# Attention transposes in 64-row halves, and a planner that counts 512-column evacuations as longer

## The chip, the cores and the metric

One core of one Trainium2 chip runs the whole program. The metric is the device time of that core in microseconds, the median of several executions.

## The reference

Causal block attention (blocks of 64) over 8 batches, 8 heads, 576 positions and head size 64, then a layer norm, a two-layer ReLU network of width 2048 and a residual, all in fp32:

```
scores = q @ k.T / sqrt(D), masked so that block i sees blocks j <= i
attn   = exp(scores - max) / (sum + 1e-9)
x      = attn @ v                       # heads side by side: 512 columns
xn     = (x - mean) / sqrt(var + 1e-6) * g_ln
out    = x + max(xn @ w_ch1, 0) @ w_ch2
```

## The kernel before, in words

**Two stages.** The attention runs over 32 pairs of heads (`pair`, line 396), with a short extra piece for the first block of every second batch (`first`, line 552, after pairs 3, 11, 19 and 27). Then the network runs over rounds of row tiles (`products` and `second`), and is one long stream of matmuls. Its weights arrive as 64-bit words, which `decode` turns into fp32 on ACT, DVE and POOL while the attention runs, and the first row tiles are normalised (`norm_tiles`, `operands`) there as well. This is the filler of DVE and ACT.

**One pair.** TensorE makes the scores of the two heads in 64-row mode, one head on the upper 64 rows of the array and one on the lower: first the small blocks into two `s1` banks (S1, 512 columns per head), then the large ones into two double banks `s` (S0, 1024 columns per head). DVE reads each score block once (line 443, a custom operation that masks, copies to SBUF and takes the row's extreme): four operations per S1 (320, 192, 320, 192 columns into `pu`), four per S0 (576 and 448 for each head into `pab`). They are called softenings here. ACT takes exponentials in place (line 446). TensorE turns the exponentials (`turn`, line 451): eight cells of 128x128 of `pu` in two banks, sixteen of `pab` in four banks, four cells to a bank. Each bank is then copied to SBUF by DVE or ACT (`evac`, line 387; the copies stand at L236 for DVE and L234 for ACT) into `pt1` and `pt0`. Then the products with V follow (`pv`, lines 461 and 465): PV1 reads `pt1`, PV0 reads `pt0`, both write bank `o`, which DVE transposes out (line 539, `ot`).

**PSUM.** The `s1`, transposed, `o` and `p` tiles share four banks under one tag, `tr`, and take them in turn: per pair two for `s1`, six for the transposes, one for `o`. The `s` tiles have four banks of their own.

**What sets the order.** `Plan` (line 61) is a list scheduler that runs when the program is built. Every piece of work is a task with a cost per engine; some may go to DVE or ACT (`any_of`), and it takes the engine that it expects to be done first. Its output is a fixed order per engine; at run time an engine waits where a semaphore says so. The attention's TensorE work is put in one fixed chain by `pe(at, phase, ...)` and `plan.chain`: in step k come S1(k), S0(k), then the transposes of pair k-1 for `pt1` (T1) and `pt0` (T0), then PV1(k-1) and PV0(k-1). A 512-column evacuation is counted by `dve(n)` and `act(n)`:

```
def dve(n):
    return .07 + n / 960
def act(n, sbuf=False):
    return .055 + .085 * sbuf + n / 1200
```

The planner's cost of one transposed cell is .112 (`4 * .112` per bank), and `SWITCH` adds a cost when TensorE changes between 128-row work, 64-row work and the column halves of the V products.

Of the kernel before, what the change touches and what calls it, by code (L numbers as in the profile page):

```python
# [18 lines left out]
P = 128  # L19
# [4 lines left out]
BIAS = {'PE': 0, 'SP': 0, 'DVE': 0, 'ACT': 0, 'POOL': 0}  # L24
WARM = 12
MMO = .0134
ROUNDS = 8, 8, 8, 8, 4
TILES = sum(ROUNDS)
D_0, D_1 = 12.0, .97
# [28 lines left out]
class Plan:  # L58
# [5 lines left out]
    def add(self, eng, cost=None, fn=None, r=(), w=(), prio=0.0, size=0, alloc=(), mode=128):  # L64
        k = Task(eng if isinstance(eng, dict) else {eng: (cost, fn)}, prio, size)
        k.mode = mode
        before = {}
        for x in r:
            before.update(dict.fromkeys(x.writers))
        for x in w:  # L70
            before.update(dict.fromkeys(x.readers))
        for x in r:
            x.readers.append(k)
        for x in w:
            x.writers.append(k)
        for x in before:
            x.next.append(k)
        k.left = len(before)
        k.uses = list(dict.fromkeys(x.root for x in (*r, *w, *alloc)))
        for x in k.uses:  # L80
            x.users += 1
        k.allocs = [x for x in dict.fromkeys(x.root for x in (*w, *alloc)) if x.make]
        self.tasks.append(k)
        return k
# [105 lines left out]
# [6 lines that stand above are left out]
# [6 lines left out]
def attn_mlp_kernel(ctx: ExitStack, tc: tile.TileContext, qk, qk0, v, v0, w1, w2, g, out):  # L202
# [8 lines left out]
    nc = tc.nc  # L211
# [12 lines left out]
    add = plan.add  # L224
# [3 lines left out]
    def any_of(fn, **costs):  # L228

        return {e: (c, lambda e=e: fn(engines[e])) for e, c in costs.items()}  # L230

    def copy(e, out, in_):
        if e is nc.scalar:
            e.copy(out=out, in_=in_)  # L234
        else:
            e.tensor_copy(out, in_)  # L236
# [37 lines left out]
    new_tr, new_s1, new_o, new_p = (kind(n, [P, 512], F32, 4, psum, "tr") for n in ("tr", "s1", "o", "p"))  # L274
# [37 lines left out]
    ident = odd.tile([P, P], F32, name="ident")  # L312
# [72 lines left out]
    HALF = slice(0, 64), slice(64, 128)  # L385

    def evac(out, in_, n, **kw):
        add(any_of(lambda e: copy(e, out(), in_()), DVE=dve(n), ACT=act(n)), **kw)

    def pe(at, phase, *args, **kw):  # L390
        steps.setdefault((at, phase), []).append(add("PE", *args, **kw))
# [3 lines left out]
    def pair(k):  # L395
        b, c = k // 4, k % 4
        prio = 100 + 10 * k
        step = [0]

        def pr():  # L400
            step[0] += 1
            return prio + .05 * step[0]
# [5 lines left out]
        else:  # L408
            early, late = Buf(parent=raw), Buf(parent=raw)
            for to, at, boxes in ((early, 30, ((slice(0, P), 0, 64, 320), (HALF[0], 1, 256, 576), (HALF[1], 1, 0, 320))),  # L410
                                  (late, 20, ((slice(0, P), 0, 320, 576), (HALF[0], 1, 0, 256), (HALF[1], 1, 320, 576)))):
                for rows, m, lo, hi in boxes:
                    load((rows.stop - rows.start) * (hi - lo) * 4, lambda rows=rows, m=m, lo=lo, hi=hi: nc.sync.dma_start(
                        out=raw.t[rows, m, lo:hi], in_=qk[k][rows, m, lo:hi]), w=[to], alloc=[raw], prio=prio - at)
# [12 lines left out]
        def cell(i, h, ck):  # L427

            at = FIRST[i] + (128 * i if ck == 0 else 128 * (i + ck) if h else 128 * (i - ck))
            return slice(at, at + P)  # L430
# [20 lines left out]
        def turn(o, slots):  # L451

            def go():
                for n, x in enumerate(slots()):
                    nc.tensor.transpose(o.t[:, n * P:(n + 1) * P], x, ident)  # L455
            return go

        def pv(o, at, z, steps):
            def go():
# [12 lines left out]
        pu = new_pu()  # L472
# [6 lines left out]
        low = [[], []]  # L479
# [5 lines left out]
        pab = big_of[k, 0] = new_pab()  # L485
# [8 lines left out]
        done = [[], []]  # L494
# [3 lines left out]
        pt0 = big_of[k, 1] = new_pt0()  # L498
        final[k] = [*done[0], *done[1]]
        got = []  # L500

        for h in range(2):
            for i in (4, 3):
                o, x = new_tr(), Buf(parent=pt0)
                if i == 4:
                    cells = [(4, h, ck) for ck in range(1, 5)]
                    need = [done[h][0]]
                else:
                    cells = [(3, h, ck) for ck in range(1, 4)] + [(3 + h, h, 0)]
                    need = [done[h][1]] + [done[x][1 - h] for x in range(2)]  # L510
                slots = lambda cells=cells: [pab.t[:, cell(*x)] for x in cells]
                pe(k + 1, 3, 4 * .112, turn(o, slots), r=list(dict.fromkeys(need)), w=[o], alloc=[pt0], prio=pr())
                evac(lambda h=h, i=i: pt0.t[:, h, :, i - 3], lambda o=o: o.t.rearrange("p (c n) -> p c n", c=4), 512,
                     r=[o], w=[x], prio=pr())
                got.append(x)
        ob, part_o = new_o(), []
        part_o.append(Buf(parent=ob))
        pe(k + 1, 5, (4 * 256 + 128) * 4 / 2400 + .06, pv(
# [2 lines left out]

        pt1 = new_pt1()
        got = []
        for h in range(2):
            o, x = new_tr(), Buf(parent=pt1)

            cells = (1, h, 1), (2, h, 1), (1 + h, h, 0), (2, h, 2)
            slots = lambda cells=cells: [pu.t[:, cell(*x)] for x in cells]
            need = low[h] + [low[x][1 - h] for x in range(2)]
            pe(k + 1, 2, 4 * .112, turn(o, slots), r=list(dict.fromkeys(need)), w=[o], alloc=[pt1], prio=pr())  # L530
            evac(lambda h=h: pt1.t[:, h].rearrange("p c i n -> p (c i n)"), lambda o=o: o.t, 512, r=[o], w=[x], prio=pr())
            got.append(x)
        part_o.append(Buf(parent=ob))
        pe(k + 1, 4.5, (2 * 256 + 128) * 4 / 2400 + .06, pv(
            ob, 0, lambda: pt1.t[:, :, 1, 0],
# [4 lines left out]
        rows = Buf(parent=xd[b])  # L540
# [98 lines left out]
    n = 0  # L639
# [388 lines left out]
```

## Time and profile before

| what | value |
|---|---|
| median of 3 runs | 1050.25 us (1049.67 to 1051.68) |
| span of the profiled execution | 1051.5 us (no other time of it is listed) |
| TensorE (PE) busy | 99% |
| VectorE (DVE) busy | 71% |
| ScalarE (ACT) busy | 50% |
| GpSimd (POOL) busy | 27% |
| mean granted TensorE clock | 0.996 |

The page's busy share of PE says that it almost never sits idle; it doesn't say whether its order could be shorter. The slices of the page show two different stages: over the first third ACT and DVE are at 7 to 9 tenths, afterwards at 2 to 4 and 5 to 6. So the stages have to be read apart, the first one step by step.

### The profile page before, as it was taken

How to read it: one execution, taken by the hardware profiler on the slowest of the kernel's cores; microseconds unless marked ns; L12 is line 12 of the kernel's file. 1: busy time of each engine (PE TensorE's matmuls, PEld its weight loads, DVE VectorE, ACT ScalarE, POOL GpSimd, SP SyncE). 2: the span in 40 equal slices, each digit the busy share in tenths (PEclk: the TensorE clock that was granted, in tenths of full speed). 3: DMA queues.
4: the chain of work that ended last, by engine and by line, in shares of the span. 5: the costliest groups of instructions: out<-in, count | busy, mean ns of one | idle time of the engine just before them, and what ended most of it. 6: DMA issues, size and time to landing. Idle time of an engine off the chain costs nothing.

```text
span 1051.5 us, 18007 instructions
## 1 busy us (share of the span) xinstructions
PE 1039.6 (99%) x6264; PEld 855.0 (81%) x6264; DVE 743.6 (71%) x1631; ACT 525.0 (50%) x1264; POOL 285.8 (27%) x468
## 2 busy tenths in 40 slices
PE   9999999999999999999999999999999999999998
PEld 7887777777778888888888888888888888888997
DVE  5878999789978878885656694665685565465544
ACT  7999897889984544441433341343242322122221
POOL 0223354445433755340222240222231220000000
PEclk9999999999999999999999999999999999999999
DMA  7678889898779898758787747688657667336873
GB/s 274 205 252 265 223 282 258 226 288 291 282 255 293 299 324 240 231 215 255 225 254 208 220 179 252 186 233 261 182 190 260 217 190 248 143 111 246 299 282 123
DMA packets 238682, 248.88 MB, mean 237 GB/s; under 512 B 159488, under 2 KB 189184, under 8 KB 228352
## 3 DMA queue, kind: packets, MB, share of 16 engines
q1 hardware_dynamic: 238592, 247.74, 73.1%
q8 instruction: 49, 0.80, 0.3%
q14 instruction: 41, 0.34, 0.1%
HBM read 182.68 MB, written 65.01 MB: 236 GB/s over the span
## 4 chain that ended last, share of the span: by engine, by line
PE 90%; DVE 6%; DMA 2%; ACT 1%; issue 1%; SPq 0%; POOL 0%; DVEq 0%; ACTq 0%; POOLq 0%
PE y L938 36%; PE p L876 32%; PE tr L455 7%; PE s L425 7%; PE o L465 5%; PE o L461 3%; DVE pab L443 1%; DMA x<-xd 1%; DMA was<-wa 1%; DVE pu L443 0%; DMA xrow<-x 0%; DVE ya L950 0%; DVE x L733 0%; DVE x L678 0%; DVE sgn L359 0%
## 5 line engine op out<-in xcount | busy, mean ns | idle before, releaser
L938 PE MATMUL y<-wc,h 128*128 128x512 f32 (+1 forms) x1740 | 434.0, 388 | 0.2 <-DVE h L896 0.2
L938 PEld LDWEIGHTS y<-wc,h 128*128 128x128 f32 x1740 | 323.0, 188 | 66.1 <-DVE h L896 1.3
L950 DVE TENSOR_TENSOR ya<-y,ya 128x512 f32<-128x512 f32 x290 | 198.0, 684 | 183.6 <-PE y L938 182.1
L876 PE MATMUL p<-xm,wa 128*128 128x512 f32 (+1 forms) x960 | 221.7, 368 | 0.0
L876 PEld LDWEIGHTS p<-xm,wa 128*128 128x128 f32 x960 | 169.9, 188 | 31.5 <-issue 0.2
L876 PE MATMUL p<-xm,wb 128*128 128x512 f32 (+1 forms) x720 | 166.3, 368 | 0.0
L884 ACT COPY t<-p 128x512 f32<-128x512 f32 (+1 forms) x120 | 65.3, 544 | 168.6 <-PE p L876 166.8
L876 PEld LDWEIGHTS p<-xm,wb 128*128 128x128 f32 x720 | 127.7, 188 | 23.6
L895 ACT ACTIVATE h<-t 128x512 fp32r<-128x512 f32 (+1 forms) x120 | 62.2, 579 | 163.5 <-DVE t L889 163.2
L889 DVE TENSOR_TENSOR t<-p,t 128x512 f32<-128x512 f32 (+1 forms) x120 | 76.3, 636 | 48.1 <-PE p L876 43.3
L425 PE MATMUL s<-raw 64*128 64x224 f32 (+3 forms) x768 | 97.6, 389 | 1.7 <-DVE nm L443 1.2
L234 ACT COPY pt<-tr 128x512 f32<-128x512 f32 x166 | 87.4, 597 | 9.1 <-PE tr L455 8.0
L446 ACT ACTIVATE pab<-pab,nm 128x448 f32<-128x448 f32 (+1 forms) x128 | 91.1, 730 | 0.1
L425 PEld LDWEIGHTS s<-raw 64*128 64x128 f32 x768 | 75.3, 189 | 17.8 <-issue 5.0
L443 DVE CUSTOM_DVE_ANT_0 pab<-s,never 128x448 f32<-128x448 f32 (+1 forms) x128 | 82.7, 684 | 2.5 <-PE s L425 1.9
L465 PE MATMUL o<-pt,v 128*64 128x256 f32 (+1 forms) x768 | 80.6, 345 | 0.0
L465 PEld LDWEIGHTS o<-pt,v 128*64 128x64 f32 x768 | 55.7, 138 | 28.3 <-issue 1.1
L896 DVE SCALAR_TENSOR_TENSOR h<-t,h 128x512 fp32r<-128x512 f32 (+1 forms) x120 | 74.1, 668 | 3.9 <-ACT h L895 3.8
L353 POOL TENSOR_SCALAR mag<-mag 128x512 f32<-128x512 f32 x32 | 48.7, 1523 | 100.0 <-ACT mag L350 92.1
L690 POOL TENSOR_SCALAR norm<-norm 128x1 f32<-128x1 f32 x28 | 7.2, 258 | 248.9 <-ACT xn L687 248.9
L446 ACT ACTIVATE pu<-pu,nm 128x320 f32<-128x320 f32 (+1 forms) x128 | 64.7, 509 | 19.9 <-DVE nm L443 18.9
L455 PE MATMUL tr<-ident,pab 128*128 128x128 f32 x512 | 65.0, 279 | 5.1 <-DVE nm L443 4.2
(96 smaller groups left out, 1035.6 us busy)
## 6 DMA issues: line engine op xcount, KB each, us to landing
wc<-wcs SPq DMA_DIRECT2D x40, 1024.0 KB, 7.1
wa<-was SPq DMA_DIRECT2D x32, 1024.0 KB, 6.4
wb<-wbs SPq DMA_DIRECT2D x32, 768.0 KB, 5.5
raw<-qk SPq DMA_DIRECT2D x31, 576.0 KB, 4.9
wr<-w SPq DMA_DIRECT2D x32, 512.0 KB, 6.2
v<-v SPq DMA_DIRECT2D x32, 320.0 KB, 5.2
x<-xd SPq DMA_DIRECT2D x144, 64.0 KB, 4.0
xrow<-x SPq DMA_DIRECT2D x36, 256.0 KB, 4.2
```

The source lines that it names most:

```text
L234: e.copy(out=out, in_=in_)
L425: nc.tensor.matmul(x, raw.t[HALF[h], 0, col], raw.t[HALF[h], 1, at:at + x.shape[1]], start=True, stop=True)
L443: add("DVE", dve(n) + .01, lambda: nc.vector.tensor_tensor_reduce(out=two(p.t[:, part(i, h)]), in0=mine(), in1=two(hide), scale=-0.125, sc ...
L446: add("ACT", act(n, True) + .14, lambda: nc.scalar.activation(out=p.t[:, part(i, h)], in_=p.t[:, part(i, h)], func=AF.Exp, bias=nm.t[:, at ...
L455: nc.tensor.transpose(o.t[:, n * P:(n + 1) * P], x, ident)
L465: nc.tensor.matmul(o.t[HALF[h], at + lo:at + 256], v_sb.t[:, ck, HALF[h]], rhs(h), start=False, stop=(n == len(steps) - 1), skip_group_che ...
L876: nc.tensor.matmul(x.t[:, 0:TN], w_(l), xs[m].t[:, 0:half, o, k], start=start and k == e == 0, stop=k == 1 and e == 2, skip_group_check=True)
L884: add("ACT", act(TN), lambda: nc.scalar.copy(out=t.t[:, 0:TN], in_=x.t[:, 0:TN]), r=[r], w=[new], prio=0)
L889: add("DVE", dve(TN), lambda: nc.vector.tensor_add(t.t[:, 0:TN], x.t[:, 0:TN], t.t[:, 0:TN]), r=r, w=[new], prio=0)
L896: add("DVE", dve(TN), lambda: nc.vector.scalar_tensor_tensor(out=x.t[:, 1, 0:TN], in0=src(), scalar=0.0, in1=x.t[:, 0, 0:TN], op0=ALU.max, ...
L938: nc.tensor.matmul(yb.t[:, cut], x.t[:, l, at:at + P], wc.t[:, i, o, cut], start=i == e == 0, stop=i == 1 and e == 2, skip_group_check=end)
L950: add("DVE", dve(cut.stop - cut.start), lambda yb=yb, ya=ya, cut=cut: nc.vector.tensor_add(ya.t[:, cut], yb.t[:, cut], ya.t[:, cut]), r=[p ...
```

## The change

The transposes go over to half cells. Each 128x128 cell becomes two matmuls in 64-row mode: the upper 64 rows (64 queries) times a 64x64 identity into one bank, the lower 64 rows into another, 64 columns each. A bank now holds one half of eight cells, so a group of eight cells fills two banks together, and there are three groups per pair: `pu` (T1), head 0 of `pab` (T0a) and head 1 (T0b). The copies still read 512 columns each, six per pair, and write runs of 64 columns. For the planner, a group costs 8 cells at .112 and is in mode 64 like the scores, and a 512-column evacuation lasts .08 (DVE) or .115 (ACT) longer than before. These costs enter the choice between DVE and ACT, and with it the order of everything else on the two engines.

```diff
 MMO = .0134
+TURN = .112
@@
     def evac(out, in_, n, **kw):
-        add(any_of(lambda e: copy(e, out(), in_()), DVE=dve(n), ACT=act(n)), **kw)
+        add(any_of(lambda e: copy(e, out(), in_()), DVE=dve(n) + .08, ACT=act(n) + .115), **kw)
@@
             def go():
                 for n, x in enumerate(slots()):
-                    nc.tensor.transpose(o.t[:, n * P:(n + 1) * P], x, ident)
+                    for rows, to in zip(HALF, o):
+                        nc.tensor.transpose(to.t[:, 64 * n:64 * n + 64], x[rows], ident[rows, rows])
             return go
+
+        def turned_to(pt, at, o, x, to):
+            for q, src in enumerate(o):
+                x.append(Buf(parent=pt))
+                evac(lambda q=q: to()[..., 64 * q:64 * q + 64],
+                     lambda src=src: src.t.rearrange("p (c i q) -> p c i q", c=4, q=64), 512, r=[src], w=[x[-1]], prio=at)
@@
         for h in range(2):
-            for i in (4, 3):
-                o, x = new_tr(), Buf(parent=pt0)
...
-                pe(k + 1, 3, 4 * .112, turn(o, slots), r=list(dict.fromkeys(need)), w=[o], alloc=[pt0], prio=pr())
-                evac(lambda h=h, i=i: pt0.t[:, h, :, i - 3], lambda o=o: o.t.rearrange("p (c n) -> p c n", c=4), 512,
-                     r=[o], w=[x], prio=pr())
-                got.append(x)
+            o = [new_tr(), new_tr()]
+            cells = [x for c in range(3) for x in ((3, h, c + 1), (4, h, c + 1))] + [(3 + h, h, 0), (4, h, 4)]
+            slots = lambda cells=cells: [pab.t[:, cell(*x)] for x in cells]
+            need = [*done[h], done[1 - h][1 - h]]
+            pe(k + 1, 3, 8 * TURN, turn(o, slots), r=list(dict.fromkeys(need)), w=o, alloc=[pt0], prio=pr(), mode=64)
+            turned_to(pt0, pr(), o, got, lambda h=h: pt0.t[:, h])
@@
-        for h in range(2):
-            o, x = new_tr(), Buf(parent=pt1)
...
+        o = [new_tr(), new_tr()]
+        cells = [x for h in range(2) for x in ((1, h, 1), (2, h, 1), (1 + h, h, 0), (2, h, 2))]
+        slots = lambda: [pu.t[:, cell(*x)] for x in cells]
+        pe(k + 1, 2, 8 * TURN, turn(o, slots), r=[*low[0], *low[1]], w=o, alloc=[pt1], prio=pr(), mode=64)
+        turned_to(pt1, pr(), o, got, lambda: pt1.t.rearrange("p h c i n -> p (h c) i n"))
```

Over the whole program the planner gives DVE 67 of the 196 evacuations where it had 30, and ACT 129 where it had 166. TensorE gets 1,536 transposes of 128x64 (128 output partitions, 64 columns) in place of 768 of 128x128. Three places show what moved.

TensorE, step 17 of the attention, from the last scores to the first products with V (first before, then changed; `x8` counts like instructions, `s<-raw` are scores, `o<-pt` products with V):

```order
L425 MATMUL s<-raw 128x224 x4
L455 MATMUL tr<-ident,pu 128x128 x8
L455 MATMUL tr<-ident,pab 128x128 x16
L461 MATMUL o<-pt_2161,v 64x256 x2
L465 MATMUL o<-pt_2161,v 64x256 x2
```

```order
L426 MATMUL s<-raw 128x224 x4
L457 MATMUL tr<-ident,pu 128x64 x16
L457 MATMUL tr<-ident,pab 128x64 x32
L469 MATMUL o<-pt_2558,v 64x256 x2
L473 MATMUL o<-pt_2558,v 64x256 x2
```

The chain is the same; each transpose has become two of half the columns.

DVE, the same step 17, the softenings of S0 and what stands around them (first before, then changed; `ISA pab` is a softening, `ISA nm` its row extreme, `COPY pt` an evacuation, `sgn` and `wd` weight decoding):

```order
L443 ISA pab,nm<-s,never 128x576
L443 ISA nm 128x1
L443 ISA pab,nm<-s,never 128x448
L443 ISA nm 128x1
L443 ISA pab,nm<-s,never 128x576
L443 ISA nm 128x1
L236 COPY pt_2178<-tr 128x4x128
L443 ISA pab,nm<-s,never 128x448
L443 ISA nm 128x1
L359 SCALAR_TENSOR_TENSOR sgn<-wr,sgn 128x512
L362 SCALAR_TENSOR_TENSOR sgn<-mag,sgn 128x512
L236 CAST wd<-sgn 128x512
```

```order
L360 SCALAR_TENSOR_TENSOR sgn<-wr,sgn 128x512
L444 ISA pab,nm<-s,never 128x576
L444 ISA nm 128x1
L237 COPY pt_2558<-tr 128x8x64
L444 ISA pab,nm<-s,never 128x448
L444 ISA nm 128x1
L444 ISA pab,nm<-s,never 128x576
L444 ISA nm 128x1
L237 COPY pt_2582<-tr 128x8x64
L444 ISA pab,nm<-s,never 128x448
L444 ISA nm 128x1
L363 SCALAR_TENSOR_TENSOR sgn<-mag,sgn 128x512
```

DVE has one evacuation among the S0 softenings before, and two in the changed order: one of T1 (`pt_2558`) and one of T0 (`pt_2582`), and a piece of decoding stands ahead of them.

DVE again, step 26, from the first softening of S0 to `ot` (first before, then changed):

```order
L443 ISA pab,nm<-s,never 128x448
L443 ISA nm 128x1
L236 COPY pt_3388<-tr 128x4x128
L443 ISA pab,nm<-s,never 128x576
L443 ISA nm 128x1
L443 ISA pab,nm<-s,never 128x448
L443 ISA nm 128x1
L359 SCALAR_TENSOR_TENSOR sgn<-wr,sgn 128x512
L362 SCALAR_TENSOR_TENSOR sgn<-mag,sgn 128x512
L236 CAST wd<-sgn 128x512
L539 STREAM_TRANSPOSE ot<-o 128x512
```

```order
L444 ISA pab,nm<-s,never 128x576
L444 ISA nm 128x1
L444 ISA pab,nm<-s,never 128x448
L444 ISA nm 128x1
L444 ISA pab,nm<-s,never 128x448
L444 ISA nm 128x1
L237 COPY pt_4006<-tr 128x8x64
L444 ISA pab,nm<-s,never 128x576
L444 ISA nm 128x1
L237 COPY pt_4006<-tr 128x8x64
L536 STREAM_TRANSPOSE ot<-o 128x512
```

Here the second of two evacuations of `pt0` stands behind all four softenings; before, the only one stood behind two.

## Rows read from the trace of the kernel before

**Rows 1.** Busy time by stage (--windows): attention steps 1 to 30, and everything behind.
```profile
core 0: us, PE busy (x) PEld busy (x) DVE busy (x) ACT busy (x) POOL busy (x), PEclk, DMA share, GB/s
8.33:294.34 286.01, 279.30 (x2673) 220.14 (x2673) 246.97 (x743) 257.48 (x699) 105.88 (x134) 0.99 0.83 262
310.70:1051.50 740.80, 737.14 (x3416) 616.29 (x3414) 482.56 (x849) 250.38 (x525) 173.27 (x323) 1.00 0.70 228
```

**Rows 2.** TensorE in time (--timeline), step 17: start, length, line, tile, count.
```profile
156.18 2.86 PE L425 MATMUL s<-raw 64*128 64x320 f32 x24
158.97 1.09 PE L455 MATMUL tr<-ident,pu 128*128 128x128 f32 x8
159.90 1.91 PE L455 MATMUL tr<-ident,pab 128*128 128x128 f32 x16
161.74 0.65 PE L461 MATMUL o<-pt,v 128*64 128x256 f32 x4
162.88 0.60 PE L461 MATMUL o<-pt,v 128*64 128x256 f32 x4
163.31 1.68 PE L465 MATMUL o<-pt,v 128*64 128x256 f32 x16
164.92 2.86 PE L425 MATMUL s<-raw 64*128 64x320 f32 x24
```

**Rows 3.** Who waited for whom, 8 to 306 us: total us, times, longest.
```profile
DVE ot L539 <- PE o L465: 24.2, 21, 2.7
...
PE tr L455 <- DVE nm L443: 4.2, 3, 1.7
```

**Rows 4.** Groups by line and form: busy us, mean ns of one, idle before.
```profile
L455 PE MATMUL tr<-ident,pab 128*128 128x128 f32 x512 | 65.0, 279 | 5.1 <-DVE nm L443 4.2 <-ACT pt L234 0.6 <-DVE pt L236 0.3
...
L577 PE MATMUL tr<-qk 64*64 64x64 f32 x128 | 2.8, 224 | 0.0
...
L425 PEld LDWEIGHTS s<-raw 64*128 64x128 f32 x768 | 75.3, 189 | 17.8 <-issue 5.0 <-DVE ot L539 1.2 <-DVE nm L443 1.1
...
L236 DVE COPY pt<-tr 128x512 f32<-128x512 f32 x29 | 20.0, 689 | 9.1 <-PE tr L455 8.6 <-PE tr L606 0.2
...
L234 ACT COPY pt<-tr 128x512 f32<-128x512 f32 x165 | 86.9, 596 | 9.1 <-PE tr L455 8.0 <-issue 0.2
```

**Rows 5.** DVE in time, from step 17 into step 18.
```profile
159.07 0.76 DVE L443 CUSTOM_DVE_ANT_0 pab<-s,never 128x576 f32<-128x576 f32 x1
...
159.75 0.62 DVE L443 CUSTOM_DVE_ANT_0 pab<-s,never 128x448 f32<-128x448 f32 x1
...
160.30 0.75 DVE L443 CUSTOM_DVE_ANT_0 pab<-s,never 128x576 f32<-128x576 f32 x1
...
161.41 0.69 DVE L236 COPY pt<-tr 128x512 f32<-128x512 f32 x1 [0.35 <-PE tr L455]
162.02 0.61 DVE L443 CUSTOM_DVE_ANT_0 pab<-s,never 128x448 f32<-128x448 f32 x1
...
162.56 0.69 DVE L359 SCALAR_TENSOR_TENSOR sgn<-wr,sgn 128x512 int32<-128x512 int32 x1
...
165.04 0.72 DVE L539 STREAM_TRANSPOSE ot<-o 128x512 f32<-128x512 f32 x1
166.08 0.49 DVE L443 CUSTOM_DVE_ANT_0 pu<-s,never 128x320 f32<-128x320 f32 x1 [0.33 <-PE s L425]
...
167.47 0.69 DVE L362 SCALAR_TENSOR_TENSOR sgn<-mag,sgn 128x512 int32<-128x512 int32 x1
```

**Rows 6.** ACT in time, step 17: four evacuations in one row.
```profile
159.72 2.05 ACT L234 COPY pt<-tr 128x512 f32<-128x512 f32 x4
```

**Rows 7.** Busy time (--windows, columns as in rows 1) of two long steps, 19 and 20.
```profile
173.66:187.11 13.45, 11.40 (x115) 8.47 (x113) 9.82 (x32) 9.10 (x27) 6.00 (x17) 0.87 1.01 343
187.11:200.05 12.94, 11.06 (x86) 8.38 (x80) 10.26 (x31) 9.59 (x23) 6.46 (x5) 0.87 0.73 164
```

More of the change, by code (lines that the diff above doesn't have):

```diff
@@ L502, in pair @@
         for h in range(2):
-            for i in (4, 3):
-                o, x = new_tr(), Buf(parent=pt0)
[L505 to L511, printed above, removed]
-                pe(k + 1, 3, 4 * .112, turn(o, slots), r=list(dict.fromkeys(need)), w=[o], alloc=[pt0], prio=pr())
-                evac(lambda h=h, i=i: pt0.t[:, h, :, i - 3], lambda o=o: o.t.rearrange("p (c n) -> p c n", c=4), 512,
-                     r=[o], w=[x], prio=pr())
-                got.append(x)
+            o = [new_tr(), new_tr()]
[4 more added lines that the diff above has]
+            turned_to(pt0, pr(), o, got, lambda h=h: pt0.t[:, h])
         ob, part_o = new_o(), []
@@ L523, in pair @@
         got = []
-        for h in range(2):
-            o, x = new_tr(), Buf(parent=pt1)
[L527 to L532, printed above, removed]
+        o = [new_tr(), new_tr()]
[3 more added lines that the diff above has]
+        turned_to(pt1, pr(), o, got, lambda: pt1.t.rearrange("p h c i n -> p (h c) i n"))
         part_o.append(Buf(parent=ob))
```

## The prediction

> **What bounds the kernel now.** I read the stages first. Behind the attention TensorE is busy for 737.14 of 740.80 us [rows 1], so the end moves by what the attention gains or loses. Steps 1 to 30 of the attention take 286.01 us [rows 1], 9.53 each.
>
> Then one step in time [rows 2]. Step 17 lasts 8.74 us (156.18 to 164.92) and TensorE goes through it without a gap: scores 2.79, transposes 2.77, PV1 1.14, PV0 2.04. PV0 starts 6.70 after the step does. This is TensorE's own pace. The thirty steps are 24 us longer than 30 x 8.74; that is the extra piece of `first` (eight steps) and steps in which DVE comes late. Steps 19 and 20 alone take 13.45 and 12.94 [rows 7], and TensorE's largest wait is for softenings, 4.2 us [rows 3].
>
> Then the two engines that feed TensorE. DVE is busy for 247 and ACT for 257 of the 286 us [rows 1], so neither has much to spare. But their instructions overlap: a DVE copy is 0.69 long and its follower starts 0.61 after it (161.41, 162.02) [rows 5]; four ACT copies take 2.05, and with 0.60 for one that is 0.48 from start to start [rows 4, 6]. In the same way a softening of 576 columns occupies DVE for 0.68, one of 448 for 0.54, the four of S1 for 1.39 (166.08 to 167.47), decoding for some 0.66 [rows 5]. DVE's largest wait is for the products with V, 24.2 us in 21 waits [rows 3]. So in a normal step TensorE bounds, with DVE close behind.
>
> **The transposes themselves.** Sixteen cells take 1.91 us, one 0.28, so a cell costs (1.91 - 0.28) / 15 = 0.109 [rows 2, 4]. A 64-column matmul is 0.224 long against 0.279 for 128 columns [rows 4]: 64 columns save 0.055 and so cost about that. Two halves in the two row halves of the array can run side by side, as the scores do: 24 matmuls of 192 to 320 columns between 156.18 and 158.97 take 0.116 each [rows 2], where one alone, at 0.109 for 128 columns, would need at least 0.16. So the bounds for a cell are 0.055 (full overlap) and 0.109 (no gain). I take 0.058, nearest to the 64-column row: 24 cells in 1.4 us in place of 2.77. The scores and transposes are now in one mode; 24 x 0.109 = 2.62 of 2.77 leaves 0.15 for the changes of mode and the first load, of which I take 0.1 off. TensorE alone would save 1.5 us a step, 44 us in all.
>
> A rule speaks against this. The Trainium skill, page "TensorE: Matmul & The Clock Gate", section Part 2 (LDWEIGHTS), says that a weight load costs by its columns and not by its rows; half cells would then need twice the load time. The trace has 768 loads of 64 rows and 189 ns that keep their port busy for only 75.3 us, 98 ns each [rows 4], so loads of two row halves overlap; by the rule without overlap the sum would be that of the last rival below.
>
> **Where the saving stops.** Three groups of eight cells fill two banks each, and there are four banks, two of which hold `s1` until it is softened. So T0b cannot start before both copies of T1 are out, and PV0 not before the last copy. I walk step 17 in its changed order, from the start of S1. The S1 softenings start at 1.16 (166.08 - 164.92) and end at 2.55 [rows 2, 5]. The piece of decoding now ahead of S0's brings 3.21 (without it they would start at 2.89, as 159.07 - 156.18). Then 0.68 to 3.89, the T1 copy to 4.50, 0.54, 0.68 to 5.72, and the T0 copy to 6.33 [rows 5]; its data is out 0.08 later, and with the signal PV0 starts at 6.46. ACT, with four copies of 0.48 [rows 6], is through at 5.8. T0b runs from 4.6 to 5.1 and PV1 from 5.2 to 6.35, both in time. PV0 takes 2.04: the step lasts 8.50, not 7.2. The gain is 0.24.
>
> In step 26 DVE has all four softenings and two copies of T0 behind each other: 2.89 + 0.68 + 0.54 + 0.54 + 0.61 + 0.68 + 0.61 = 6.55, PV0 at 6.69, the step 8.73: no gain. From the first S0 softening to the last copy DVE now needs 3.0 to 3.3 us in ten of the thirty steps, about 3.7 in ten, 4.7 in one, and under 2.6 in nine, where ACT's copies or work ahead of the softenings decide.
>
> **The load.** DVE gets 37 evacuations more, 37 x 0.61 = 22.6 us; ACT loses 37 x 0.48 = 17.8. With what else changes place (three more weight words are decoded before the last `ot`, some casts go to ACT and POOL, which is at 106 of 286 us [rows 1] and costs nothing), DVE's own work in steps 1 to 30, by the counts of the two orders and the start-to-start times, goes from 234 to 251 us. No transfer is added. To the 251 come two waits that the chain forces on DVE in each step: 2.55 to 2.89, and about 0.4 between `ot` and the next S1 softening. That is 251 + 30 x 0.75 = 274, the floor for the thirty steps.
>
> **The sum.** I added up all thirty steps like step 17: PV0 starts at the latest of TensorE's own chain (6.1 now, 6.70 before), DVE's and ACT's; a DVE that ends a step late starts the next one late; `first` adds 0.6 to 1.1 in eight steps. This gives 269 for the order before, against 286.0 measured, and 276 for the changed one. Of the 17 that it misses before, 8.3 are in steps 19 and 20, where the granted clock was 0.87 [rows 7]: 0.13 x 26.4 = 3.4 us by the clock, the rest by late softenings, which in the changed order are already in the 276. I add 3.4 for the clock, 2.4 for the slow first step, 2 for small waits: 284, a gain of 2. At the end two more transposes are shorter by 1.4 each, and the order fills TensorE's waits there with products of the network: 2.5. Together 4.5 off the profiled 1051.5, so 1047.0; the median of the runs stands 1.25 below that profile. I predict **1046**.
>
> **The rivals.**
> - Forecast, a small gain: TensorE's saving is caught by the DVE chain, with 2 to 8 us left. For it: PV0 at 6.46 and 6.69 in the two walks. Against: the walk missed 17 us before. Chance 0.40.
> - A larger gain: waits overlap better and the steps reach DVE's floor, 274 - 286 = -12, with 3 at the end: about 1036. Against: every filler would have to fit. Chance 0.10.
> - No change: more steps go like step 26, and the walk's gain is lost in small waits, 1048.2 to 1052.3. (A measurement can tell about 0.2%, 2.1 us.) This is also what comes if half cells cost 0.109: T0b then ends near 5.5, PV0 moves to some 6.6. Chance 0.19.
> - Slower by DVE: it has 17 us more to do and becomes the bound. The point is where DVE's step, 8.36 on average plus 0.75, passes TensorE's, and that is near. If the walk misses as much as before, 276 + 17 = 293, 7 us more, with 2.5 back at the end: 1055. Chance 0.21.
> - Slower by the clock: a step whose transposes wait for late softenings falls to the 1.2 GHz level, as between 173.66 and 200.05 [rows 7], at 0.13 x 13 = 1.7 us each. In the changed order four more steps (those behind `first`) have late softenings: 7 us, which turns the gain into 1053. The Trainium skill, page "TensorE: Matmul & The Clock Gate", section Part 4, says that transposes do not count as activity for the clock; by that rule the waits now among the transposes would lengthen such stretches, and the trace agrees so far that the clock fell where transposes waited. Chance 0.07.
> - Loads one after the other: 2 x 0.11 a cell makes 24 cells 5.3 us; PV0 could start at about 8.9, 2.2 late, 66 us in all: 1116. The overlap of the score loads speaks against it. Chance 0.03.
>
> **How the numbers follow.** Faster: 0.40 + 0.10 = 0.50; same: 0.19; slower: 0.21 + 0.07 + 0.03 = 0.31. The range goes from the floor, 1036, to 1059, which takes in both slower cases but the last and leaves something for both together. The forecast's own range is 1042 to 1048.
>
> **What the profile after will show.** If I am right: transposes near 0.058 a cell, waits of TensorE for copies (`pt` on DVE and ACT) in most steps where there were none, PV0 starting 6.1 to 6.8 after S1, the thirty steps within 5 us of 286, DVE's wait for the products with V smaller. A cell at 0.109, steps of 7.5 us, a clock under 0.95 over the attention, or a network stage with waits would each show a step of this wrong; steps well over 9.5 us with DVE never waiting would show the slower case.

## The result, and the profile after

The changed kernel takes 1056.83 us (median of 4 runs, 1055.12 to 1058.84) against 1050.97 for the kernel before (4 runs): a ratio of 1.0061, 95% interval 1.0042 to 1.0081. It is slower by about 6 us, where 4 us faster was forecast. The time is inside the range, with the wrong sign.

The page of the changed kernel, engine totals (busy us, share of the span, instructions):

```profile
span 1054.3 us, 19524 instructions
...
PE 1017.6 (97%) x7032; PEld 834.1 (79%) x7032; DVE 759.7 (72%) x1654; ACT 508.0 (48%) x1233; POOL 284.1 (27%) x476
```

TensorE's share falls from 99% to 97%: its work shrank, the span did not, and what it saved is now waiting.

A second profile of the kernel before (run before_again) matters for what follows. Its span is 1048.3, that of the first was 1051.5, and in every profile here whose run has a time, that time is 1.8 to 2.1 us above the span. So the first one stood some 3 us above the median of 1050.25. The difference is in steps 19 and 20, which took 13.45 and 12.94 at a clock of 0.87 there [rows 7]. In the second profile the same two steps (--windows, columns as in rows 1):

```profile
174.06:184.64 10.58, 9.83 (x114) 7.40 (x113) 9.47 (x32) 8.06 (x24) 6.53 (x17) 1.00 1.03 368
184.64:195.97 11.33, 9.44 (x87) 7.30 (x81) 10.27 (x31) 9.27 (x24) 6.47 (x5) 1.00 0.83 222
```

Against that second profile the comparison by stage is clean. Busy time by stage, steps 1 to 30 and everything from the last S1 on; first the kernel before (second profile), then the changed one:

```profile
core 0: us, PE busy (x) PEld busy (x) DVE busy (x) ACT busy (x) POOL busy (x), PEclk, DMA share, GB/s
8.27:291.11 282.84, 276.68 (x2672) 217.99 (x2672) 246.97 (x743) 256.66 (x700) 105.70 (x134) 1.00 0.83 265
291.11:1048.30 757.19, 753.51 (x3558) 628.76 (x3556) 493.99 (x879) 264.56 (x560) 180.84 (x328) 1.00 0.70 228
```

```profile
8.51:296.60 288.09, 257.85 (x3393) 202.13 (x3393) 256.73 (x761) 244.62 (x678) 107.43 (x138) 0.99 0.83 261
296.60:1054.30 757.70, 753.37 (x3606) 626.60 (x3604) 499.62 (x881) 260.12 (x550) 176.02 (x333) 1.00 0.70 228
```

Of the 6.0 us between these two spans 5.25 are in the thirty steps, 0.5 behind them, 0.24 ahead. TensorE is busy 19 us less in the thirty steps, and idle for 30 in place of 6. (The work saved is more than these 19: in step 17 below, T0b takes 0.98 for what T1 does in 0.66, and counts as busy throughout.) Ten steps of the kernel before run at TensorE's 8.74, in both profiles; only three of the changed kernel's are as short (8.50, 8.58, 8.58).

Which waits these are (the view of waits, TensorE in the attention, 8 to 306 us: total us, times, longest):

```profile
PE tr L457 <- ACT pt L235: 17.6, 36, 1.0
PE o L469 <- ACT pt L235: 3.3, 8, 0.5
PE tr L457 <- DVE pt L237: 2.1, 3, 0.8
...
PE o L469 <- DVE pt L237: 1.4, 4, 0.7
```

Transposes wait for copies 39 times; the kernel before had hardly any such wait [rows 4]. Step 17, walked in the prediction, shows one. TensorE in time (start, length, line, tile, count, idle before), from S1 at 157.10 to the next at 166.56:

```profile
157.10 2.86 PE L426 MATMUL s<-raw 64*128 64x320 f32 x24
159.80 0.66 PE L457 MATMUL tr<-ident,pu 64*128 64x64 f32 x16
160.29 0.22 PE L457 MATMUL tr<-ident,pab 64*128 64x64 f32 x1
160.66 0.72 PE L457 MATMUL tr<-ident,pab 64*128 64x64 f32 x15
162.28 0.98 PE L457 MATMUL tr<-ident,pab 64*128 64x64 f32 x16 [0.90 <-ACT pt L235]
163.18 0.65 PE L469 MATMUL o<-pt,v 128*64 128x256 f32 x4
163.67 0.82 PE L473 MATMUL o<-pt,v 128*64 128x256 f32 x8
164.46 0.65 PE L469 MATMUL o<-pt,v 128*64 128x256 f32 x4
```

T1 takes 0.66 in place of 1.09, then T0b (162.28) waits until ACT has copied one of T1's two banks; DVE copies the other from 161.81 on, and T0b takes 0.98 where T1 took 0.66. ACT could not do so earlier. ACT and DVE in the same step:

```profile
159.67 0.56 ACT L447 ACTIVATE pu<-pu,nm 128x320 f32<-128x320 f32 x1 [0.90 <-DVE nm L444]
...
161.22 0.44 ACT L447 ACTIVATE pu<-pu,nm 128x192 f32<-128x192 f32 x1
161.57 0.19 ACT L447 ACTIVATION_READ_ACCUMULATOR pu<-pu,nm 128x1 f32 x1
161.66 2.16 ACT L235 COPY pt<-tr 128x512 f32<-128x512 f32 x4
```

```profile
156.58 1.12 DVE L363 SCALAR_TENSOR_TENSOR sgn<-mag,sgn 128x512 int32<-128x512 int32 x1
157.62 0.70 DVE L735 STREAM_TRANSPOSE xnt<-x 128x512 f32<-128x512 f32 x1
158.25 0.67 DVE L536 STREAM_TRANSPOSE ot<-o 128x512 f32<-128x512 f32 x1
158.85 0.38 DVE L237 CAST wd<-sgn 128x512 fp32r<-128x512 f32 x1
159.16 0.47 DVE L444 CUSTOM_DVE_ANT_0 pu<-s,never 128x320 f32<-128x320 f32 x1
...
161.81 0.68 DVE L237 COPY pt<-tr 128x512 f32<-128x512 f32 x1
```

The chain reads backwards: T0b at 162.28 waits for the first of four ACT copies (161.66), which stand behind four exponentials of S1 (from 159.67), which waited 0.90 for the S1 softenings, and these start at 159.16, 2.06 after S1, because DVE was still at a decode, a transpose of `x`, `ot` and a cast. The prediction had them start 1.16 after S1. PV0 starts at 164.46, 7.36 after S1, where 6.46 was predicted: late by the same 0.90.

### The profile page after: what moved, and what is told of

Same layout as the page of the kernel before. It is cut to its first block, busy times and chain, and to the rows that moved or that the text cites. A ratio compares the mean times of both kernels' runs of the same rounds, so it can differ in the third digit from the quotient of the medians.

```text
span 1054.3 us, 19524 instructions
## 1 busy us (share of the span) xinstructions
PE 1017.6 (97%) x7032; PEld 834.1 (79%) x7032; DVE 759.7 (72%) x1654; ACT 508.0 (48%) x1233; POOL 284.1 (27%) x476
## 4 chain that ended last, share of the span: by engine, by line
PE 72%; DVE 3%; ACT 1%; issue 0%; DVEq 0%; ACTq 0%
PE y L935 36%; PE p L873 32%; PE o L473 1%; PE s L426 1%; PE o L469 1%; PE tr L457 1%; DVE ya L947 1%; DVE xm L771 0%; DVE pab L444 0%; ACT pt L235 0%; ACT pu L447 0%; DVE h L893 0%; DVE xm L237 0%; ACT pab L447 0%; DVE pt L237 0%; DVE t L886 0%
## 5 line engine op out<-in xcount | busy, mean ns | idle before, releaser
L447 ACT ACTIVATE pab<-pab,nm 128x576 f32<-128x576 f32 (+1 forms) x128 | 91.3, 721 | 1.5 <-DVE nm L444 1.3
L473 PEld LDWEIGHTS o<-pt,v 128*64 128x64 f32 x768 | 60.1, 138 | 24.1 <-issue 1.2
L893 DVE SCALAR_TENSOR_TENSOR h<-t,h 128x512 fp32r<-128x512 f32 (+1 forms) x120 | 76.4, 685 | 3.8 <-ACT h L892 3.8
L447 ACT ACTIVATE pu<-pu,nm 128x192 f32<-128x192 f32 (+1 forms) x128 | 63.8, 500 | 30.2 <-DVE nm L444 28.2
L457 PE MATMUL tr<-ident,pab 64*128 64x64 f32 x1024 | 53.3, 228 | 22.5 <-ACT pt L235 17.6
L235 ACT COPY pt<-tr 128x512 f32<-128x512 f32 x129 | 68.3, 580 | 2.9 <-PE tr L457 2.2
L457 PEld LDWEIGHTS tr<-ident,pab 64*128 64x128 f32 x1024 | 42.3, 139 | 32.3 <-ACT pt L235 22.6
```

The lines of the kernel that those rows point to most:

```text
L447: add("ACT", act(n, True) + .14, lambda: nc.scalar.activation(out=p.t[:, part(i, h)], in_=p.t[:, part(i, h)], func=AF.Exp, bias=nm.t[:, at ...
L457: nc.tensor.transpose(to.t[:, 64 * n:64 * n + 64], x[rows], ident[rows, rows])
L473: nc.tensor.matmul(o.t[HALF[h], at + lo:at + 256], v_sb.t[:, ck, HALF[h]], rhs(h), start=False, stop=(n == len(steps) - 1), skip_group_che ...
L893: add("DVE", dve(TN), lambda: nc.vector.scalar_tensor_tensor(out=x.t[:, 1, 0:TN], in0=src(), scalar=0.0, in1=x.t[:, 0, 0:TN], op0=ALU.max, ...
```

## The experiments

"DVE" is how many of the 196 evacuations the plan gives to DVE; "thirty" and "behind" are the time of steps 1 to 30 and from the last S1 to the end, in the one profiled execution of each run. Times are medians; the kernel before had 1050.0 to 1050.4 in each group of experiments, and 1051.0 beside the changed kernel. The profiled execution is not always a typical one: that of half_act and that of full_jit stood 4 us above the median (1064.2 and 1058.1), those of early_new and early_fast_new 2 us above it, that of group_only 2.7 below (1058.9), so their "thirty" and "behind" are uncertain by as much.

| run | DVE | us | ratio to before (95%) | thirty | behind |
|---|---|---|---|---|---|
| before (before_again) | 30 | 1050.1 | | 282.8 | 757.2 |
| changed | 67 | 1056.8 | 1.0042 to 1.0081 | 288.1 | 757.7 |
| half_old | 61 | 1058.0 | 1.0057 to 1.0086 | 289.4 | 758.3 |
| full_new | 70 | 1058.3 | 1.0055 to 1.0081 | 284.4 | 761.9 |
| half_fast | 72 | 1048.8 | 0.9977 to 1.0010 | 276.6 | 761.3 |
| early_new | 67 | 1046.2 | 0.9937 to 0.9972 | 279.6 | 758.0 |
| half_act | 33 | 1060.0 | 1.0084 to 1.0135 | 296.7 | 757.4 |
| early_old | 66 | 1058.9 | 1.0074 to 1.0103 | 287.2 | 761.9 |
| early_fast | 65 | 1049.1 | 0.9981 to 1.0016 | 267.1 | 771.1 |
| full_early | 14 | 1057.8 | 1.0062 to 1.0087 | 287.7 | 759.7 |
| full_jit | 44 | 1054.0 | 1.0025 to 1.0056 | 288.7 | 759.3 |
| half_jit | 69 | 1061.2 | 1.0095 to 1.0121 | 291.8 | 758.7 |
| half_fast_new | 72 | 1055.7 | 1.0034 to 1.0067 | 283.4 | 761.6 |
| after_whole | 67 | 1062.8 | 1.0089 to 1.0133 | 292.6 | 758.5 |
| early_whole | 67 | 1058.5 | 1.0052 to 1.0092 | 290.1 | 757.5 |
| fast_whole | 72 | 1057.6 | 1.0046 to 1.0088 | 285.2 | 762.3 |
| early_fast_new | 81 | 1054.6 | 1.0022 to 1.0057 | 274.2 | 771.9 |
| group_only | 71 | 1061.7 | 1.0095 to 1.0129 | 291.7 | 757.1 |

**First, the two parts of the change apart, and two cures.** half_old keeps the half transposes and takes the planner's longer evacuation costs back; full_new has those costs alone:

```diff
-DVE=dve(n) + .08, ACT=act(n) + .115
+DVE=dve(n), ACT=act(n)
```

> The half transposes alone: the planner's evacuation costs are as before the change (a 512-column copy at .603 on DVE and .482 on ACT). The plan then gives DVE 61 of the 196 evacuations, against 67 in the changed kernel and 30 before. Theory A (the longer costs mislead the planner: the two copy engines start a copy every .61 and .48, so a copy counted as .68 and .60 makes it see engines fuller than they are, and this is what costs the 6 us): about 1048 to 1051, no slower than before. Theory B (the transposes in two-bank groups cost it: T0b waits for the copies of T1): 1056 to 1058, as the changed kernel, with TensorE's waits of transposes for copies near 20 us as in the changed profile. Theory C (the planner counts a cell as .112 where .0625 is measured, and puts the fillers of DVE and ACT to a wrong timetable): also about 1056.

> The kernel before with the planner's longer evacuation costs alone; transposes in whole cells of 128 columns. DVE gets 70 evacuations, more than in the changed kernel. Theory A: slower than before by most of the 6 us, 1055 to 1058, with more DVE work (70 - 30) x .61 = 24 us in the attention. Theory B and C: within 2 us of before, 1049 to 1053, because DVE's extra copies fit into its idle time (39 of 286 us before).

Measured: 1058.0 and 1058.3. Each half of the change alone costs nearly 8 us, and both together cost 6. None of A, B and C foresaw both. full_new also tells where: its thirty steps are 1.6 longer with 70 copies on DVE, and 4.7 us are lost behind them, where products of the network wait 2.4 us for `h` and the granted clock is 0.97 between 420 and 470 us.

half_fast is half_old with the measured cell in the plan, early_new is the changed kernel with T1 between S1 and S0:

```diff
-TURN = .112
+TURN = .063
```

```diff
-pe(k + 1, 2, 8 * TURN, turn(o, slots), r=[*low[0], *low[1]], ...
+pe(k + 1, .5, 8 * TURN, turn(o, slots), r=[*low[0], *low[1]], ...
```

> Half transposes, evacuation costs as before, and a cell of two halves counted as .063 as measured in the changed profile in place of .112. DVE gets 72 evacuations. Theory C: the plan now has the true timetable of TensorE, 1046 to 1050. Theory B: 1055 to 1058, the waits for T1's copies stay (40 us in all before transposes). Theory A: as half_old, 1048 to 1051.

> The changed kernel with one thing moved: T1 stands between S1 and S0 in TensorE's chain in place of between S0 and T0a, so that its two copies go on while TensorE makes the scores of S0 (1.7 us) and its two banks are free when T0b wants them. Evacuation costs and the cell cost are those of the changed kernel; DVE has 67 evacuations as there. Theory B: the waits of transposes for copies by ACT (17.6 us in 36 waits in the changed kernel) nearly go, and the time falls by 8 us or more, to 1049 or less. Theory A and C: 1055 or more, since costs and timetable are the same. A risk for all: S1's banks are still held when T1 comes early, so T1 needs the other two, and PV1's bank o comes later; if this binds, it is slower than 1058.

Measured: 1048.8, as theory C had it, and 1046.2, as theory B had it. The view of waits of early_new (as above) says why B is nevertheless not the whole of it:

```profile
PE o L469 <- ACT pt L235: 12.8, 28, 0.9
PE o L469 <- DVE pt L237: 5.0, 11, 2.3
...
PE tr L457 <- ACT pt L235: 1.2, 3, 0.5
```

The transposes hardly wait for ACT's copies any more (17.6 to 1.2). But the products with V now wait for copies, 17.8 us in place of 4.7. TensorE arrives earlier at the same bound, the last copies of the step.

**Second, the same cures on other orders, and DVE's load.** half_act makes the planner see DVE's copy .2 longer:

```diff
-DVE=dve(n), ACT=act(n)
+DVE=dve(n) + .2, ACT=act(n)
```

early_old, early_fast and full_early move T1 as early_new does, in half_old, in half_fast and in the kernel before.

> Half transposes with the planner's DVE copy counted .2 longer and its ACT copy as before the change: DVE then gets 33 of the 196 evacuations, nearly the 30 of the kernel before, against 61 in the run half_old that differs in this alone (1058.0 us). Theory D (the extra copies on DVE are the cost: 28 x .61 = 17 us of DVE work less here): about 1050. Theory B (the transposes of T0b wait for banks whichever engine copies): 1056 to 1060, with TensorE's waits for copies by ACT above the 16.4 + 4.2 us of half_old, since ACT now copies nearly all.

> The run half_old (half transposes, evacuation costs as before the change, cell counted as .112) with T1 moved between S1 and S0, as early_new did to the changed kernel. DVE gets 66 evacuations, ACT 130. Theory B (bank waits of T0b): falls from 1058.0 by 8 to 12, to 1046 to 1050. A theory that early_new's 1046.2 came from a lucky order and not from the banks: within 3 us of 1058.

> Both: T1 between S1 and S0, and a cell counted as .063 as measured; evacuation costs as before the change. DVE gets 65 evacuations. If the bank waits (B) and the planner's timetable (C) are separate causes, this is below either alone (early_new 1046.2, half_fast 1048.8): about 1040 to 1044. If they are one cause seen twice: 1045 to 1049.

> The kernel before, with whole cells of 128 columns, and T1 moved between S1 and S0: tells whether moving T1 helps by itself. Here a group fills one bank and no transpose waited for a copy of T1 (the largest wait of transposes for copies in the kernel before was under 2 us), and TensorE changes its row mode twice more a step. Theory B: 1050 to 1056, no gain or a loss by the mode changes. If it gains as much as early_new did (10 us), to about 1042, then the move is good whatever the transposes are, and the bank waits are not what it cured.

Measured: 1060.0, 1058.9, 1049.1 and 1057.8. half_act speaks against D: with 33 copies on DVE it is no faster than with 61, where D had it at 1050, so the number of copies there does not make the loss. early_old speaks against B as the whole cause: the same move that took 10.7 us off in early_new adds 0.9 here. Its attention is 2.2 shorter (287.2 against 289.4 in half_old), and 3.6 are lost behind it. full_early: with whole cells the move costs 7.7, more than theory B allowed for. TensorE waits for only 5 us there in the attention; its steps without waits take 9.09 (as from 17.32 to 26.41) in place of 8.74, the same cells with two more changes of mode.

early_fast is the surprise. Its thirty steps take 267.1, 16 less than before, and almost none of that reaches the end: 771.1 behind the last S1 in place of 757.2. TensorE's waits there (300 to 470 us), the window 400 to 460 (columns as in rows 1), and DVE in time:

```profile
PE y L935 <- ACT h L892: 5.9, 2, 4.2
PE y L935 <- DVE h L893: 3.8, 2, 3.5
```

```profile
400.00:460.00 60.00, 50.38 (x202) 40.03 (x201) 51.22 (x93) 23.92 (x50) 34.56 (x43) 0.92 0.79 251
```

```profile
396.95 0.68 DVE L947 TENSOR_TENSOR ya<-y,ya 128x512 f32<-128x512 f32 x1
402.33 0.43 DVE L760 TENSOR_TENSOR tt<-xt 128x256 f32<-128x256 f32 x1 [4.70 <-DMA w1f<-sgn]
402.67 0.68 DVE L947 TENSOR_TENSOR ya<-y,ya 128x512 f32<-128x512 f32 x1
403.27 0.42 DVE L760 TENSOR_TENSOR tt<-xt,tt 128x256 f32<-128x256 f32 x1
403.60 0.70 DVE L735 STREAM_TRANSPOSE xnt<-x 128x512 f32<-128x512 f32 x1
404.23 0.65 DVE L886 TENSOR_TENSOR t<-p,t 128x512 f32<-128x512 f32 x1
```

and ACT:

```profile
404.92 1.67 ACT L892 ACTIVATE h<-t 128x512 fp32r<-128x512 f32 x3 [6.52 <-DVE t L886]
```

DVE stands for 4.70 us in front of an operand of the next round (`tt`), put down to a DMA; `ya` and the `t` of the products that TensorE needs stand behind it in DVE's order, and ACT's `h` waits 6.5 us for that `t`. The clock is 0.92 in that window; the kernel before has 59.83 us of TensorE work and 1.00 in the same stretch. In this order, time won in the attention arrives at a network whose operands are not ready.

**Third, is it the change, or any change of the order?** full_jit and half_jit alter one planner cost by 3%, in the kernel before (at each place where it stands, the piece of `first` included) and in the changed one; half_fast_new is the changed kernel with `TURN = .063`; before_again was read above.

```diff
-4 * .112
+4 * .109
```

```diff
-TURN = .112
+TURN = .109
```

> The kernel before with the planner's cost of a transposed cell at .109, as measured before the change, in place of .112: a change of 3% in one cost, and no other. It moves a large part of the rows of DVE's order; DVE gets 44 evacuations in place of 30. Theory E (the list scheduler's order scatters: any small change of costs loses some 7 us against an order whose constants were chosen for it, and what the change, half_old, full_new and full_early lost is mostly that): 1055 to 1059. If the order doesn't scatter, and the losses of those runs are each their own mechanism: 1048 to 1052.

> The changed kernel with a cell counted as .109 in place of .112, and no other edit; DVE gets 69 evacuations in place of 67. Theory E: anywhere from 1048 to 1060, and the distance to the changed kernel's 1056.8 is the size of the scatter. Theory C (the planner's timetable, whose cell should be .063): within 2 us of 1056.8, as a step from .112 to .109 is 6% of the way.

> The changed kernel with a cell counted as .063 as measured (half_fast with the longer evacuation costs). Theory C: as in the pairs half_old to half_fast and early_old to early_fast (9 to 10 us less each), 1046 to 1050, by a thirty-step stretch of some 276 in place of 288 us. If it stays at 1055 or more, the cell cost doesn't act by itself.

> The kernel before, unchanged, for a second profile. The first one's span of 1051.5 is, with the 1.9 us between a span and the time of its run that every other profile here shows, some 3 us above the median of the runs of before. If steps 19 and 20 (13.45 and 12.94 there) are that execution's own, they take about 9 to 10 here, and the thirty steps some 283 us in place of 286.

Measured: 1054.0 (+3.6), 1061.2 (+4.3 on the changed kernel), 1055.7, and for the kernel before 10.58, 11.33 and 282.8. So the order scatters: a cost that moves by 0.003 moves the time by about 4 us, in both cases upward. Theory E's kind is right; both times lie 1 us outside its ranges, and two draws don't tell how far the scatter goes. Theory C shortens the thirty steps in all pairs, half_old to half_fast by 12.8, early_old to early_fast by 20.1, the changed kernel to half_fast_new by 4.7, early_new to early_fast_new by 5.4; the end moves by -9.2, -9.8, -1.1 and +8.4. As a statement on the end it falls; as one on the attention it holds.

**Fourth, the order held.** after_whole, early_whole and fast_whole put whole cells back into the changed kernel, early_new and half_fast, and leave every row of DVE, ACT, POOL and SP in its place:

```diff
-for rows, to in zip(HALF, o):
-    nc.tensor.transpose(to.t[:, 64 * n:64 * n + 64], x[rows], ident[rows, rows])
+nc.tensor.transpose(o[n // 4].t[:, n % 4 * P:n % 4 * P + P], x, ident)
@@
-evac(lambda q=q: to()[..., 64 * q:64 * q + 64],
-     lambda src=src: src.t.rearrange("p (c i q) -> p c i q", c=4, q=64), ...
+evac(lambda q=q: to()[:, 2 * q:2 * q + 2],
+     lambda src=src: src.t.rearrange("p (c i n) -> p c i n", c=2, n=P), ...
```

early_fast_new is early_new with `TURN = .063`. group_only is after_whole with the evacuation costs of before and the transposes planned as 128-row work, so the kernel before with nothing of the change but eight cells to a group of two banks.

> The changed kernel with whole cells of 128x128 in place of the halves (a group of eight cells still fills two banks, now four whole cells each) and every instruction of DVE, ACT, POOL and SP in the same order as in the changed kernel. So only the transposes differ: this measures what half cells are worth in a fixed order. If TensorE's saving reached the end in full, 24 x (.109 - .0625) = 1.1 us a step would come back, 33 us in all: 1090. If DVE and ACT's chain of softenings and copies bounds most steps (Theory F), most of the longer transposes fills TensorE's waits (30 us in the changed kernel's attention): 1057 to 1070. If the halves in themselves cost time: below 1055.

> The same for the fastest order so far (early_new, 1046.2): whole cells, the order of the other engines unchanged. Theory F: 1050 to 1062, a loss of a third or less of the 33 us. Full saving: 1079. Here TensorE also changes its row mode twice more a step than before the change.

> The same for the order of half_fast (1048.8), which was planned for cells of .063: whole cells in it. Since that plan puts the softenings and copies as close behind the transposes as half cells allow, the loss should be the largest of the three if the planner's timetable is what counts (Theory C): 1065 to 1082. Theory F alone: as the other two, 1052 to 1064.

> A candidate for the fastest: T1 between S1 and S0, a cell counted as .063, an evacuation with the longer cost. The run early_fast, which differs in the evacuation costs alone, had the shortest attention (267 us for the thirty steps, against 283 before) but lost it in the network, where TensorE then waited 10 us for late operands (1049.1). If the fillers decide (the work of DVE that no longer fits beside the attention comes late in the network): 1044 to 1052 here too, whatever the attention takes. If that was an accident of one order: 1036 to 1042.

> The kernel before, whole cells and all planner costs as there, with one thing of the change alone: eight cells to a group that fills two banks together, so that both copies of a group come ready at once. DVE gets 71 of the 196 evacuations. If the grouping makes the loss that the half cells then partly win back (after_whole 1062.8 against before 1050.1): 1056 to 1064. If the costs alone make it (full_new 1058.3): 1049 to 1053.

Measured: 1062.8, 1058.5, 1057.6, 1054.6 and 1061.7. In a fixed order half cells gain 6.0 us (1062.8 to 1056.8), 12.3 (1058.5 to 1046.2) and 8.8 (1057.6 to 1048.8). They are good in all three, and all three whole times lie in theory F's ranges. In early_whole the whole cells also bring two more changes of mode to each step. fast_whole was not the largest loss, against theory C. early_fast_new fits neither of its two ranges. And the grouping alone, in whole cells and with the order that the planner makes of it, costs 11.7. So the change loses 12.7 by its new order (after_whole over before: grouping, longer costs and transposes planned in mode 64), and half cells win 6.0 back. Within the 12.7 the parts don't add up: grouping alone 11.7, costs alone 7.9, each with another order, and the scatter of orders is in all three.

TensorE's waits for copies in group_only (8 to 306 us):

```profile
PE tr L456 <- ACT pt L235: 1.4, 2, 1.0
PE o L468 <- DVE pt L237: 1.4, 5, 0.4
PE tr L456 <- DVE pt L237: 1.1, 2, 0.8
PE o L468 <- ACT pt L235: 1.0, 4, 0.3
```

That is 4.9 us where the kernel before has 0.9 [rows 4], so 4.0 of the 8.9 by which this attention is longer; what makes the rest is open.

What half cells could give is seen where a step runs with hardly a wait. TensorE's transposes and the steps' length in early_whole (step from 101.97 to 111.06, 9.09) and early_fast_new (66.70 to 74.45, 7.75):

```profile
103.04 1.09 PE L456 MATMUL tr<-ident,pu 128*128 128x128 f32 x8
...
105.99 1.97 PE L456 MATMUL tr<-ident,pab 128*128 128x128 f32 x16
```

```profile
67.67 0.66 PE L457 MATMUL tr<-ident,pu 64*128 64x64 f32 x16
...
69.94 1.17 PE L457 MATMUL tr<-ident,pab 64*128 64x64 f32 x32
71.27 0.65 PE L469 MATMUL o<-pt,v 128*64 128x256 f32 x4 [0.16 <-ACT pt L235]
```

The second step as a whole (--windows, columns as in rows 1):

```profile
66.70:74.45 7.75, 7.59 (x107) 6.02 (x105) 7.46 (x24) 7.60 (x21) 2.73 (x2) 1.00 0.74 225
```

9.09 - 7.75 = 1.34 a step, 40 us in thirty. But 0.35 of the 9.09 are the two changes of mode that whole cells bring with T1 early. Against the 8.74 of the kernel before TensorE saves 8.74 - 7.59 = 1.15 a step, 34 us in thirty. Of these 34 to 40 us 6 to 12 come through.

**The version that beats both** is early_new: 1046.2 us, 0.9937 to 0.9972 of the kernel before. It is half cells, longer costs and T1 early. Since early_old and early_fast_new, which differ from it in the evacuation costs alone and in the cell's cost alone, take 1058.9 and 1054.6, it is a good draw of the order as much as a good design; what exactly makes it the best isn't settled.

## Why the prediction was wrong

- **The cell: right; the saving made of it: too large.** 0.058 predicted; T1's 16 halves give (0.66 - 0.22) / 7.5 = 0.059, and T0's 32 halves (1.17 - 0.22) / 15.5 = 0.061. But TensorE saves 1.15 a step (34 us in thirty), where 1.5 (44) was predicted. From the start of T1 to that of S0, and from the start of T0 to its end, the transposes take 0.49 + 1.17 = 1.66 us; 24 cells of 0.06 are 1.44. The 0.15 beyond the cells, of which the prediction took 0.1 off, is still there (0.22).
- **Loads one after the other: refuted.** The group of the loads in the changed kernel (busy us, mean ns of one, idle before):

```profile
L457 PEld LDWEIGHTS tr<-ident,pab 64*128 64x128 f32 x1024 | 42.3, 139 | 32.3 <-ACT pt L235 22.6 <-DVE pt L237 2.9 <-DVE nm L444 2.3
```

  1,024 loads keep their port busy for 42.3 us, 41 ns each: those of the two row halves overlap. The Trainium skill, page "TensorE: Matmul & The Clock Gate", section Part 3 (what overlaps and what doesn't), says that a load overlaps with running matmuls only where the row group differs. The trace shows loads of different row groups overlapping one another, 139 ns for one and 41 ns of port time each; that "only" there is an overlap no run here shows. The price of this rival was also too low: 2.79 + 5.3 + 1.14 puts PV0 at 9.2 after S1, not 8.9, which makes 75 us and not 66.
- **Where the saving stops: right in kind.** T0b waits for the copies of T1, the products for the last copies; 6 of 34 us come through in the changed order. But the walk of step 17 let DVE begin as early as in the kernel before, 1.16 after S1. In the trace it begins 0.90 late, ACT's copies stand behind the exponentials as well, and the step takes 9.46 in place of 8.50.
- **The sum: this is the step that failed.** The walk gave 269 for the order before and 276 for the changed one, 7 us more. The text then added 17 to the first, to meet the profile, and only 8 to the second, on the grounds that late softenings were "already in the 276". That turned +7 into -2. Measured, the walk misses 282.8 - 269 = 14 and 288.1 - 276 = 12: nearly the same. The bare difference, +7, was close to the measured +5.3. That it comes so close is in part luck, since the walk put step 17, the one it shows, at 8.50, and it took 9.46.
- **The anchor.** 3.2 of the 17 were one execution's own: steps 19 and 20 of the first profile. The changed kernel's profile also has one step at 0.87 (12.72 us), so it was wrong to take such a step from the kernel before alone.
- **The end: wrong by 3.** "2.5" was to be gained behind the thirty steps; 0.5 was lost.
- **The clock: no.** 0.99 over the thirty steps, as in the first profile of the kernel before (the second has 1.00). Nor does the wait that this rival names bring the clock down by itself: in step 20 of the kernel before the transposes wait 1.64 us for softenings in the first profile and 1.65 in the second, and the twelve cells behind it take 2.45 us in the one and 1.53 in the other.
- **Slower by DVE: its price was right, its mechanism wasn't.** 1055 was close, but DVE does 256.7 us in place of 247.0 (10 more, not 17), half_act with 33 copies on DVE is no faster (1060.0), and full_new with 70 lengthens the attention by only 1.6. Nor did DVE stop waiting for the products with V, as that rival had it (8 to 306 us; 24.2 in 21 waits before [rows 3]):

```profile
DVE ot L536 <- PE o L473: 19.1, 14, 2.5
```

  What the waits show is the order around the copies: two copies of a group come ready together, and the transposes two banks later, or the products, wait for both. group_only shows that the grouping costs 11.7 in one order; how much of that is the scatter of orders (3.6 to 4.3 for a 3% cost) and how much the banks is left open.

## What to carry to other kernels

When a walk is calibrated on the kernel before, give its miss to the kernel after as well, in full, unless a row excludes it: a correction that differs between the two is a forecast of its own. Where a list scheduler sets the order, a change is two changes; hold the order and exchange the operation alone (as after_whole does) to see what it is worth, and nudge one cost by 3% to see how far the order alone moves the time. And a gain ahead of a stage counts only if that stage's operands are ready earlier too.

## What the runs showed that was not expected

- Two more changes between 64-row and 128-row work in a step cost 0.35 us: a step without waits takes 9.09 in full_early and in early_whole, and 8.74 in the kernel before, with the same cells.
- Two executions of one kernel differ by 3.2 us in the thirty steps, and by 4.5 in two of these (26.4 against 21.9), with a clock of 0.87 in the one and 1.00 in the other.
- The fastest attention (267.1) and the fastest kernel (279.6) are different orders, 12.5 us apart in the attention, and the shorter one loses 13 behind it.
